# The opening, three seams and the late chunks of a gated two-branch attention kernel dealt anew

## The chip, the cores and the metric

The kernel runs on one core of a Trainium2 chip. Its time is the device time of one execution in microseconds (us), given as the median of several runs. The engines are TensorE (PE, with PEld for its weight loads), VectorE (DVE), ScalarE (ACT), GpSimd (POOL), and SyncE (SP), from whose queue most DMAs are issued.

## The reference

Two attention branches read the same 2048 tokens of width 640 (32 heads of 20) and are mixed by a gate per token.

```python
# first branch: linear attention with softmax features
q, k, v = split_heads(x @ wqkv)
pq, pk = q @ w_phi[h], k @ w_phi[h]                 # 20 x 20 for each head
phi_q = concat(softmax(pq), softmax(-pq))           # phi_k likewise
kv = einsum('sf,sd->fd', phi_k, v); z = phi_k.sum(over s)
a = merge((phi_q @ kv) / (phi_q @ z + 1e-6)) @ A_wo

# second branch: 4 segments of 512 tokens, in order, for each head
p = softmax(q_s @ k_s.T * 20**-0.5 + mask)          # masked where the key comes after the query
phi = lambda t: where(t > 0, t + 1, exp(t))
mem = (phi(q_s) @ M) / (phi(q_s) @ zm + 1e-6)
o_s = sigmoid(beta) * mem + (1 - sigmoid(beta)) * (p @ v_s)
M += phi(k_s).T @ v_s; zm += phi(k_s).sum()
b = merge(o) @ B_wo

g = sigmoid((x * gate_w).sum(-1))
out = g * a + (1 - g) * b                           # 2048 x 640, bf16
```

## The kernel before

A *chunk* is 128 tokens (16 of them), a *half* is 320 of the 640 columns, that is 16 heads: one PSUM bank of float32. The order of instructions on PE, ACT, DVE, POOL and on SP's queue is written out by hand: an engine works through its list in program order, and what stands behind a waiting instruction waits too. Tiles come from pools with a fixed number of slots; a new tile takes the slot that was given back first, and its first writer waits until the readers of the tile before it are done.

*Opening.* The key weights and `w_phi` are folded into one matrix `WkA`: PE transposes the key weights (`emit_foldT`, L173, five groups of five), a block-diagonal `Wphi` is made from `w_phi` and a mask (`emit_Wphi`, L163, five products on DVE), and six products for each of five row blocks (`emit_foldM`, L180) give `WkA`. The tokens must lie transposed: chunks 0 to 3 go through PE (`emit_xT`, L191), the rest through transposing DMAs (`emit_xturn`). The fold's results and the transposed tokens are copied from PSUM by ACT and DVE. POOL meanwhile makes masks and fills `kvn` and `kvd`.

*Key stage* (`emit_a1`, L225, 16 chunks): PE multiplies a chunk by `WkA` (`pk`) and by the value weights (`pv`, with the gate's sum as column 321), ACT takes exp(pk) and exp(-pk) and copies pv, DVE sums and inverts over each head's 20, POOL multiplies (`EkSn`), and a DMA lays the result out in `Z` for the sums z. Then come the fold of the query weights, the sums `kv` over all chunks (L373) and their masked copies `kvn`, while DVE adds the 32 rows of `Z` (`emit_zadd`).

*Query stage* (`emit_pq`, L388): two blocks of 1024 tokens, five product groups of 128 columns each, two slots of PSUM banks wide, exps of both signs by ACT into `Eq`. After the first block PE turns the summed `Z` (`emit_z`, L259) and DVE folds it into `kvd` (`emit_zz`). `kvd` holds for each row block the z values and a column of ones: its product with `Eq` is the numerator's denominator and the softmax's own sum in one. It keeps the 13 heads that a row block touches, and a chunk's denominators take six products of 8 to 24 columns for each sign. Between the fourth and the fifth product group of the second block stand the denominators of chunks 0 to 3 (`den0`), the gate's sigmoid, and two chains of reciprocals and products (`den_chain`), first for chunk 0, then for chunks 1 to 3.

*Numerators* (from L570): for each chunk and sign six products give the numerators (`emit_num`), DVE scales them (`emit_tt`), POOL adds both signs (`oA`, L593), and a transposing DMA puts the result into `oTA` (L606) as weights for the output projection. Denominators of the next four chunks are computed ahead. Between the two signs PE also projects halves of the second branch's keys, queries and values (`emit_next_half`, L566: 32 halves, one at each place until they are used up; ACT copies them to their stages at L552). A key or query chunk of two halves is then turned by a transposing DMA (`emit_turn`). PSUM is dealt as three slots for projections (`pps`), one for denominators (`dps`) and one for each sign's numerators (`nps`).

*Second branch*: 16 double steps, four in each of four segments, each for two groups of four heads. Called d0 to d15 here. A double step has five *bursts*: score products in PSUM (L669), their exponentials on ACT (L673), and the causal zeroing on POOL (`triangles`, L680). Between bursts PE works through a list made from `PLAN`, one letter for one item:

- `h`: a half of the next segment's keys, queries or values, 5 products of 320 columns (L857), copied by DVE (L863)
- `o`: a half of the first branch's output for a chunk from `EARLY` on, 5 products (L803); `f`: a half of the final output. For a chunk below `EARLY` it has 10 products, both branches in one sum; from `EARLY` on it has 5, and DVE adds the kept first-branch half
- `A`, `B`, `C`, `D`: probabilities by values (L725), memory products (L733, L738) and their normalisation
- `x`, `y`: the second part of a feature computation for a key or query chunk (DVE, L832); `z`: turning query features; `t`: turning a chunk of the second branch's output; `u`: the last turns

A piece of `h`, `o` or `f` is one product of 320 columns, and pieces are spread over the bursts by weight. A finished key or query chunk queues its feature exponential (L829, on ACT); the first of the waiting ones is run behind bursts 0 (keys) and 2 (queries). `PLAN` and `FINS` (the order of the final halves) stand in the diff below.

*Tail* (L929 to L988): the last four chunks' outputs, with the first branch's halves added by an identity product.

## Time and profile before

| | |
|---|---|
| runs | 330.01, 330.65, 331.93 us; median 330.65 |
| profiled execution | 330.95 us, of which 329.0 us are the span of the profile |
| granted TensorE clock, mean | 0.997 of full speed |
| instructions in the span | 9567 |
| DMA traffic | 34.21 MB, mean 104 GB/s |
| chain of work that ended last | PE 40%, ACT 18%, issue 2%, DVE 1% of the span |

The span runs from the first instruction to the last on the profiled core; 1.95 us of the execution lie around it. Engines' busy times overlap, and PE's weight loads (PEld) run beside its products. In rows of grouped instructions the part left of the bar is the work (line, engine, operation, result <- operands, shape, count), then busy time and mean length of one (ns), then the engine's idle time just before such instructions and what released most of it. In rows of the timeline the first number is the start in us, the second the length; several instructions alike in a row are one entry, and a bracket tells an idle time ahead of it and its releaser.

### The profile page before, as it was taken

How to read it: one execution, taken by the hardware profiler on the slowest of the kernel's cores; microseconds unless marked ns; L12 is line 12 of the kernel's file. 1: busy time of each engine (PE TensorE's matmuls, PEld its weight loads, DVE VectorE, ACT ScalarE, POOL GpSimd, SP SyncE). 2: the span in 40 equal slices, each digit the busy share in tenths (PEclk: the TensorE clock that was granted, in tenths of full speed). 3: DMA queues.
4: the chain of work that ended last, by engine and by line, in shares of the span. 5: the costliest groups of instructions: out<-in, count | busy, mean ns of one | idle time of the engine just before them, and what ended most of it. 6: DMA issues, size and time to landing. Idle time of an engine off the chain costs nothing.

```text
span 329.0 us, 9567 instructions
## 1 busy us (share of the span) xinstructions
PE 311.3 (95%) x3937; PEld 213.8 (65%) x3940; DVE 224.0 (68%) x449; ACT 252.7 (77%) x320; POOL 210.2 (64%) x306
## 2 busy tenths in 40 slices
PE   7899999999999999799999999999999999999994
PEld 6788877964567787455556566656556666656662
DVE  2477897997788987466768776776666666363552
ACT  3777888229755545799999999999889889889842
POOL 8378689402248889756657667676686768665640
PEclk9999999999999999999999999999999999999998
DMA  7928854692015856558231364843554584612212
GB/s 231 211 67 198 190 129 130 169 369 76 2 18 109 125 110 113 110 97 121 50 59 34 73 102 66 133 73 58 106 87 67 106 107 67 96 47 62 49 63 80
DMA packets 91814, 34.21 MB, mean 104 GB/s; under 512 B 79867, under 2 KB 91771, under 8 KB 91771
## 3 DMA queue, kind: packets, MB, share of 16 engines
q1 hardware_dynamic: 91338, 33.11, 50.1%
q8 instruction: 31, 0.51, 0.7%
q10 hardware_dynamic: 432, 0.49, 0.5%
q14 instruction: 13, 0.10, 0.1%
HBM read 6.42 MB, written 2.62 MB: 27 GB/s over the span
## 4 chain that ended last, share of the span: by engine, by line
PE 40%; ACT 18%; issue 2%; DVE 1%; POOL 0%; ACTq 0%; DVEq 0%
ACT PT L673 16%; PE st_ps L669 10%; PE proj L803 10%; PE nda L725 8%; PE proj L857 6%; PE proj L542 2%; PE nda L733 1%; PE nda L738 1%; PE num L439 1%; PE st_ps L940 1%; ACT ek L829 1%; DVE oTA L951 0%; ACT oTA L948 0%; PE nda L940 0%; DVE rec L752 0%
## 5 line engine op out<-in xcount | busy, mean ns | idle before, releaser
L673 ACT ACTIVATE PT<-st_ps 128x1024 bf16<-128x1024 f32 x160 | 154.3, 1025 | 16.0 <-PE st_ps L669 13.2
L680 POOL TENSOR_SCALAR_AFFINE_SELECT PT<-PT 128x512 bf16<-128x512 bf16 (+1 forms) x130 | 87.0, 687 | 49.3 <-ACT PT L673 49.2
L725 PEld LDWEIGHTS <-PT 128*128 128x128 bf16 x1280 | 39.8, 96 | 11.7 <-issue 8.4
L243 POOL TENSOR_TENSOR EkSn<-Ek,krec 128x1280 bf16<-128x1280 bf16 x16 | 37.7, 2370 | 12.5 <-DVE krec L242 11.9
L725 PE MATMUL nda<-vB,PT 128*128 128x21 bf16 x1280 | 42.8, 173 | 1.2 <-DVE mtmp L768 1.0
L857 PEld LDWEIGHTS <-xTf 128*128 128x128 bf16 x320 | 28.1, 97 | 17.1 <-issue 7.6
L863 DVE CAST Z<-proj 128x320 bf16<-128x320 f32 x48 | 22.8, 487 | 22.1 <-PE proj L857 21.7
L231 PEld LDWEIGHTS <-xTf 128*128 128x128 bf16 x240 | 27.1, 113 | 6.5 <-ACT xTf L196 0.9
L239 DVE TENSOR_REDUCE ksum<-Ek 128x64 f32<-128x1280 bf16 x16 | 23.6, 1475 | 9.2 <-ACT Ek L235 9.2
L669 PE MATMUL st_ps<-Z 32*128 32x512 bf16 (+3 forms) x256 | 24.7, 299 | 4.3 <-ACT PT L673 2.1
L235 ACT ACTIVATE Ek<-pk 128x640 bf16<-128x640 f32 x32 | 20.8, 702 | 10.1 <-PE pk L231 9.3
L803 PE MATMUL proj<-WkA,oTA 128*128 128x320 bf16 x160 | 27.3, 299 | 0.0
L490 DVE TENSOR_TENSOR tt<-num,rr 128x640 f32<-128x640 f32 x32 | 24.7, 801 | 3.3 <-POOL rr L484 2.0
L593 POOL TENSOR_TENSOR oA<-tt 128x640 bf16<-128x640 f32 x16 | 24.6, 1546 | 3.4 <-DVE tt L490 3.0
L669 PE MATMUL st_ps<-Eq 32*128 32x512 bf16 (+3 forms) x256 | 25.1, 299 | 1.4 <-ACT PT L673 0.8
L765 POOL TENSOR_TENSOR oB<-td 128x320 bf16<-128x320 f32 x23 | 19.8, 860 | 6.9 <-DVE td L762 5.6
L398 ACT ACTIVATE Eq<-pq 128x1024 bf16<-128x1024 f32 x20 | 19.4, 1021 | 6.2 <-PE pq L393 4.2
L439 PEld LDWEIGHTS <-Eq 128*128 128x128 bf16 x384 | 19.8, 96 | 4.7 <-issue 1.5
L393 PE MATMUL pq<-xTf,WqA 128*128 128x512 bf16 x97 | 21.9, 379 | 0.7 <-DVE zt L263 0.6
L803 PE MATMUL proj<-WvA,oT 128*128 128x320 bf16 x120 | 22.6, 300 | 0.0
L762 DVE TENSOR_TENSOR td<-nda,rec 128x640 f32<-128x640 f32 x24 | 19.8, 825 | 2.2
L857 PE MATMUL proj<-WqB,xTf 128*128 128x320 bf16 x120 | 20.9, 300 | 0.0
(150 smaller groups left out, 541.6 us busy)
## 6 DMA issues: line engine op xcount, KB each, us to landing
Z<-EkSn SPq DMA_DIRECT2D x32, 160.0 KB, 2.7
out_dram<-orow SPq DMA_DIRECT2D x10, 160.0 KB, 2.0
WvA<-in_A_wqkv_dram SPq DMA_DIRECT2D x2, 400.0 KB, 6.5
WkB<-in_B_wk_dram SPq DMA_DIRECT2D x1, 800.0 KB
WqB<-in_B_wq_dram SPq DMA_DIRECT2D x1, 800.0 KB, 7.0
WvB<-in_B_wv_dram SPq DMA_DIRECT2D x1, 800.0 KB, 10.1
WkA<-in_A_wo_dram SPq DMA_DIRECT2D x1, 800.0 KB, 11.7
WvA<-in_B_wo_dram SPq DMA_DIRECT2D x1, 800.0 KB, 12.8
```

What stands on the lines that cost most here:

```text
L231: nc.tensor.matmul(ps[:, bk, 0:n], lhsT=key_tokens(c, sc), rhs=rhs, start=(c == 0), stop=(c == KC - 1))
L239: nc.vector.tensor_reduce(out=ksum, in_=Ek.rearrange("p s (h f) -> p (s h) f", f=DH), axis=AX.X, op=ALU.add)
L243: nc.gpsimd.tensor_tensor(out=EkSn[:, sc].rearrange("p s (h f) -> p (s h) f", f=DH), in0=Ek.rearrange("p s (h f) -> p (s h) f", f=DH), in1 ...
L439: nc.tensor.matmul(ps(bk, lo, hi), lhsT=Eqs[qb, j][:, sgn, qc * P:(qc + 1) * P], rhs=kvx[:, sgn, j, lo - h0:hi - h0, :].rearrange("p h e - ...
L490: nc.vector.tensor_tensor(out=tt[:, sgn].rearrange("p (b h) d -> p b h d", b=2), in0=ps, in1=csb, op=ALU.mult)
L593: nc.gpsimd.tensor_tensor(out=oA.rearrange("p (h d) -> p h d", d=DH), in0=tt[:, 0], in1=tt[:, 1], op=ALU.add)
L669: nc.tensor.matmul(ps[:, i - i0, o:o + L - c * P], lhsT=kT[32 * i:32 * i + 32, c * P:(c + 1) * P], rhs=qT[32 * i:32 * i + 32, c * P:L], st ...
L673: nc.scalar.activation(out=PT[:, i0:i0 + 2], in_=ps, func=ACT.Exp, scale=SCALE_B)
L680: nc.gpsimd.affine_select(out=v, in_=v, pattern=[[0, n_i], [1, P]], compare_op=ALU.is_ge, fill=0.0, base=0, channel_multiplier=-1)
L725: nc.tensor.matmul(nd[:, j, i], lhsT=block(st, c)[:, i, (j - c) * P:(j - c + 1) * P], rhs=vB[:, c, 4 * st.g + i, :], start=(c == 0), stop= ...
L803: nc.tensor.matmul(ps, lhsT=oT[:, k % KC], rhs=W[:, k % KC, hs], start=(k == 0), stop=(k == n - 1))
L857: nc.tensor.matmul(ps, lhsT=xq[:, sc // 4, k, sc % 4 * P:(sc % 4 + 1) * P], rhs=W[:, k, half * 320:(half + 1) * 320], start=(k == 0), stop ...
```

## The change

- **Opening.** `emit_Wphi` goes from DVE to POOL, ahead of the fills of `kvn` and `kvd`. The transpositions (T), fold products (M) and token transpositions (X) are written out as one sequence in another order. Copies: the fold's results all by ACT (before: even ones by DVE), the token chunks by DVE (before: ACT), the weights' transposed groups by DVE but for the second (before: 0 and 2 by DVE, the others by ACT).
- **Seam of keys and queries.** `kvd` holds all 32 heads for each row block (before: 13), so a sign's denominators of a chunk are five products of 64 columns (before: six of 8 to 24), and `wmask` moves to a pool that lives longer. The turned sums of Z and the first denominators share one tile of two banks, `z_den`. The DVE work on the turned sums (`emit_zz`) is written behind the first product group of the second query block instead of ahead of it.
- **Seam of queries and numerators.** The first denominators' chain is one for four chunks up to the sum, then a reciprocal and two POOL products for chunk 0 and for chunks 1 to 3. It is written behind the last query product group. The PSUM pools are opened in another order, with a pool `last_pps` of one slot taken by every third half, beside `pps` of two.
- **Numerators.** Four more halves, key and query of chunk 4 (the first of segment 1), join the 32; one extra place for a half stands after chunks 4, 9 and 14.
- **Seam of numerators and second branch.** Key and query chunk 4 are turned and their features queued ahead of the loop; in d0 the waiting exponentials run behind bursts 2 (queries) and 3 (keys).
- **Second branch.** `EARLY` goes from 10 to 8: chunks 8 and 9 get their first-branch output halves in segment 0 (places that the four halves leave), and their final halves are of five products. `FINS` and `PLAN` are dealt to fit.

```diff
-    wmask = wq_hold.tile([P, KC, H], F32, name="wmask")
+    wmask = Aw.tile([P, KC, H], F32, name="wmask")
...
-    kvd = Aw.tile([P, 2, KC, HW, 2], BF16, name="kvd")
+    kvd = Aw.tile([P, 2, KC, H, 2], BF16, name="kvd")
...
+    def emit_Wphi(j):
+        h0, h1 = TH[j]
+        nc.gpsimd.tensor_tensor(out=Wphi[:, j, 0:h1 - h0, :],
+                                in0=Wc[:, j:j + 1, :].to_broadcast([P, h1 - h0, DH]),
+                                in1=wmask[:, j, h0:h1, None].to_broadcast([P, h1 - h0, DH]),
+                                op=ALU.mult)
+
+    for j in range(KC):
+        emit_Wphi(j)
...
-        nc.gpsimd.tensor_copy(out=kvd[:, sgn, :, :, 1], in_=wmw)
+        nc.gpsimd.tensor_copy(out=kvd[:, sgn, :, :, 1], in_=wmask)
...
-    def emit_Wphi(j):
-        h0, h1 = TH[j]
-        nc.vector.tensor_tensor(out=Wphi[:, j, 0:h1 - h0, :],
-                                in0=Wc[:, j:j + 1, :].to_broadcast([P, h1 - h0, DH]),
-                                in1=wmask[:, j, h0:h1, None].to_broadcast([P, h1 - h0, DH]),
-                                op=ALU.mult)
-
...
-        eng = nc.vector.tensor_copy if ic % 2 == 0 and dst is WkA else nc.scalar.copy
-        eng(out=dst[:, ic, :].rearrange("p (b n) -> p b n", b=2), in_=ps[:, :, 0:320])
-
-    def emit_xT(sc):
+        nc.scalar.copy(out=dst[:, ic, :].rearrange("p (b n) -> p b n", b=2), in_=ps[:, :, 0:320])
+
+    def emit_xT(sc, eng):
...
-        nc.scalar.copy(out=xq[:, sc // 4, :, sc % 4 * P:(sc % 4 + 1) * P], in_=tp)
+        eng(out=xq[:, sc // 4, :, sc % 4 * P:(sc % 4 + 1) * P], in_=tp)
...
-    def emit_z():
-        zt_ps = aps.tile([P, KC, P], BF16, name="zt_ps", tag="w2")
+    def emit_z(bank):
+        zt_ps = bank.bitcast(BF16)[:, 0:D].rearrange("p (c t) -> p c t", c=KC)
...
+        return zt_ps
+
+    def emit_zz(zt_ps):
...
-
-    def emit_zz():
...
         for sgn in range(2):
-            nc.vector.tensor_tensor(out=kvd[:, sgn, :, :, 0], in0=wmw,
-                                    in1=zcol[:, :, sgn:sgn + 1].to_broadcast([P, KC, HW]), op=ALU.mult)
+            nc.vector.tensor_tensor(out=kvd[:, sgn, :, :, 0], in0=wmask,
+                                    in1=zcol[:, :, sgn:sgn + 1].to_broadcast([P, KC, H]), op=ALU.mult)
...
-    for n in range(KC):
-        emit_foldT(wnat_k, WkT, n, nc.vector.tensor_copy if n in (0, 2) else nc.scalar.copy)
-        if n == 3:
-            for j in range(KC):
-                emit_Wphi(j)
-    for n in range(KC):
-        emit_foldM(WkT, WkA, n)
-        if n in (1, 3):
-            for sc in (n - 1, n):
-                emit_xT(sc)
+    for step in ("T0", "T1", "T2", "M0", "M1", "T3", "T4", "M2", "X0", "M3", "X1", "M4", "X2", "X3"):
+        n = int(step[1])
+        if step[0] == "T":
+            emit_foldT(wnat_k, WkT, n, nc.scalar.copy if n == 1 else nc.vector.tensor_copy)
+        elif step[0] == "M":
+            emit_foldM(WkT, WkA, n)
+        else:
+            emit_xT(n, nc.vector.tensor_copy)
...
-    def emit_pieces(ps, ch, sgn, kvx, e):
+    def emit_num(ch, sgn):
...
+        t = nps.tile([P, 2, 512], F32, name=f"num{sgn}")
...
-            nc.tensor.matmul(ps(bk, lo, hi),
+            nc.tensor.matmul(t[:, bk, (lo - 16 * bk) * DH:(hi - 16 * bk) * DH],
...
-                             rhs=kvx[:, sgn, j, lo - h0:hi - h0, :].rearrange("p h e -> p (h e)"),
-                             start=(n in FIRST) if e > 2 else (n == 0),
-                             stop=(n in LAST) if e > 2 else (n == len(PIECES) - 1))
-
-    def emit_num(ch, sgn):
-        t = nps.tile([P, 2, 512], F32, name=f"num{sgn}")
-        emit_pieces(lambda bk, lo, hi: t[:, bk, (lo - 16 * bk) * DH:(hi - 16 * bk) * DH],
-                    ch, sgn, kvn, DH)
+                             rhs=kvn[:, sgn, j, lo - h0:hi - h0, :].rearrange("p h e -> p (h e)"),
+                             start=(n in FIRST), stop=(n in LAST))
...
     def emit_den(t, ch, k):
+        qb, qc = divmod(ch, HB // P)
         for sgn in range(2):
-            emit_pieces(lambda bk, lo, hi: t[:, k, sgn, lo:hi, :].rearrange("p h e -> p (h e)"),
-                        ch, sgn, kvd, 2)
+            for j in range(KC):
+                nc.tensor.matmul(t[:, k, sgn].rearrange("p h e -> p (h e)"),
+                                 lhsT=Eqs[qb, j][:, sgn, qc * P:(qc + 1) * P],
+                                 rhs=kvd[:, sgn, j].rearrange("p h e -> p (h e)"),
+                                 start=(j == 0), stop=(j == KC - 1))
...
-    def emit_dd(uu, n):
-        dd = emit_dsum(uu, n)
-        nc.vector.reciprocal(out=dd[:, 0:n], in_=dd[:, 0:n])
-        return dd
-
-    def emit_cs(chs, rr, dd):
+    def emit_cs(chs, rr, dd, o=0):
...
-        nc.gpsimd.tensor_tensor(out=dd[:, 0:n], in0=dd[:, 0:n],
+        k = slice(o, o + n)
+        nc.gpsimd.tensor_tensor(out=dd[:, k], in0=dd[:, k],
...
-        nc.gpsimd.tensor_tensor(out=rr[:, 0:n], in0=rr[:, 0:n],
-                                in1=dd[:, 0:n, None, :].to_broadcast([P, n, 2, H]), op=ALU.mult)
-        return rr
+        nc.gpsimd.tensor_tensor(out=rr[:, k], in0=rr[:, k],
+                                in1=dd[:, k, None, :].to_broadcast([P, n, 2, H]), op=ALU.mult)
+        for i, ch in enumerate(chs):
+            cs_of[ch] = rr[:, o + i]
...
-    def den_chain(chs, dt, o):
-        rr, uu = emit_rr(dt, len(chs), o)
-        cs = emit_cs(chs, rr, emit_dd(uu, len(chs)))
-        for k, ch in enumerate(chs):
-            cs_of[ch] = cs[:, k]
+    def first_chain(dt):
+        rr, uu = emit_rr(dt, NB)
+        dd = emit_dsum(uu, NB)
+        for o, chs in ((0, [0]), (1, [1, 2, 3])):
+            nc.vector.reciprocal(out=dd[:, o:o + len(chs)], in_=dd[:, o:o + len(chs)])
+            emit_cs(chs, rr, dd, o)
...
             if (qb, j) == (0, KC - 1):
-                emit_z()
-                emit_zz()
+                z_den = w2tile("z_den")
+                zt_ps = emit_z(z_den[:, 0])
+            if (qb, j) == (1, 0):
+                emit_zz(zt_ps)
...
             if (qb, j) == (1, 3):
-                dt = w2tile("den0").rearrange("p a b -> p (a b)")[:, 0:NB * 4 * H].rearrange(
-                    "p (k s h e) -> p k s h e", k=NB, s=2, e=2)
+                dt = z_den[:, 1].rearrange("p (k s h e) -> p k s h e", k=NB, s=2, e=2)
...
-                emit_gS()
-                den_chain([0], dt, 0)
-                den_chain([1, 2, 3], dt, 1)
+    emit_gS()
+    first_chain(dt)
...
-    pps, dps, nps = [nps_stack.enter_context(tc.tile_pool(name=n, bufs=b, space=bass.MemoryType.PSUM,
-                                                          reuse_waits="tile"))
-                     for n, b in (("pps", 3), ("dps", 1), ("nps", 1))]
+    nps, dps, last_pps, pps = [nps_stack.enter_context(tc.tile_pool(
+        name=n, bufs=b, space=bass.MemoryType.PSUM, reuse_waits="tile"))
+        for n, b in (("nps", 1), ("dps", 1), ("last_pps", 1), ("pps", 2))]
...
-              for half in range(2)]
+              for half in range(2)] + [(part, 4, half) for part in "kq" for half in range(2)]
...
-            emit_half(pps, *halves.pop(0), nc.scalar.copy)
+            emit_half(last_pps if len(halves) % 3 == 1 else pps, *halves.pop(0), nc.scalar.copy)
...
+            if (ch, sgn) in ((4, 1), (9, 1), (14, 1)):
+                emit_next_half()
...
-            cs = emit_cs(ahead, rr_n, dd)
-            for n, c in enumerate(ahead):
-                cs_of[c] = cs[:, n]
+            emit_cs(ahead, rr_n, dd)
...
-        EARLY = 10
+        EARLY = 8
...
-        FIRST_SEG = [(part, c) for c in range(4) for part in "kq"]
-        FINS = [(ch, half) for ch in range(7) for half in range(2)] + [
-            (10, 0), (7, 0), (10, 1), (7, 1), (8, 0), (8, 1), (9, 0), (9, 1), (11, 0), (11, 1)]
+        FIRST_SEG = [(part, c) for c in range(1, 4) for part in "kq"]
+        FINS = [(ch, half) for ch in range(6) for half in range(2)] + [
+            (10, 0), (10, 1), (6, 0), (6, 1), (8, 0), (8, 1), (9, 0),
+            (7, 0), (9, 1), (7, 1), (11, 0), (11, 1)]
...
-        PLAN = {0: ("hhhhhhxAhD", "hhBhyhzChoxAoD", "hoBhyozChoxAoD", "hoBoyozCooxAoD"),
-                1: ("hhBhyhzChhxADtt", "hhBhyhzCfhhxAD", "hhBhyhzCfhhxADt", "hhBhyhzCfhhxAD"),
-                2: ("hhBhyhzCfhhxADt",) * 4,
-                3: ("fByfzCffADtt", "ftBfCftfAD", "fBfCftfAD", "ufBfCfffAD")}
+        PLAN = {0: ("hhhhoyzoAoxD", "hhBhyhzCooxAoD", "hhBhyhzCooxAoD", "ooBoyozCooxAoD"),
+                1: ("hhBhhChxAhDtt", "hhBhyhzCfhhxAD", "hhBhyhzCfhhxADt", "hhBhyhzCfhhxAD"),
+                2: ("hhBhyhzChxAhDt",) + ("hhBhyhzCfhhxADt",) * 3,
+                3: ("fByfzCffADtt", "fBftCfftAD", "fBftCfffAD", "ufBfCfffAD")}
...
+        for part in "kq":
+            emit_turn(part, 4, (kTs if part == "k" else qTs)[1])
+            features(part, 4)
...
-                if n in (0, 2):
-                    run_first(waiting["kq"[n == 0]])
+                if n in ((0, 2) if dstep else (2, 3)):
+                    run_first(waiting["kq"[n == (0 if dstep else 2)]])
...

```

## The prediction

> **What bounds the kernel now.** I read the page first, then busy time in stretches cut at each double step of the second branch (two head groups; d0 to d15), then the order of instructions at the seams.
>
> ```profile
> PE 311.3 (95%) x3937; PEld 213.8 (65%) x3940; DVE 224.0 (68%) x449; ACT 252.7 (77%) x320; POOL 210.2 (64%) x306
> 135.40:145.99 10.59, 9.66 (x111) 5.37 (x111) 4.85 (x11) 9.99 (x11) 5.36 (x8) 1.00 0.59 107
> 168.32:179.48 11.16, 10.62 (x158) 6.62 (x157) 8.31 (x20) 10.72 (x12) 7.23 (x13) 1.00 0.26 48
> 179.48:190.44 10.96, 10.18 (x157) 6.32 (x156) 8.14 (x18) 10.51 (x12) 7.33 (x15) 1.00 0.49 69
> 225.07:236.80 11.73, 11.48 (x172) 7.21 (x171) 7.56 (x18) 10.24 (x12) 9.03 (x17) 1.00 0.41 76
> 271.63:283.00 11.37, 11.30 (x167) 7.17 (x166) 6.30 (x14) 10.21 (x12) 9.03 (x17) 1.00 0.49 80
> 283.00:293.77 10.77, 10.64 (x157) 6.55 (x155) 4.80 (x10) 9.69 (x11) 6.45 (x11) 1.00 0.51 73
> ```
>
> The stretches read: limits, length, then PE, PEld, DVE, ACT, POOL busy, clock, DMA share, GB/s. They are d0, d3, d4, d8, d12, d13. TensorE is busy 95% overall, but the owner changes: in d3 and d4 ACT is busier than PE (10.72 against 10.62, 10.51 against 10.18), while in d8, d12 and d13 PE leads ACT by 0.95 to 1.24 us. So a product taken from d8 or d13 shortens them; in segment 0 it does not, and there an exponential counts. The clock is 1.00 throughout.
>
> **The opening.** Columns: start, length, instruction.
>
> ```profile
> 0.81 0.46 SPq L97 DMA_DIRECT2D Wc<-in_A_w_phi_dram  x1
> 2.58 0.71 POOL L141 COPY wmw<-wmask 128x12 f32<-128x12 f32 x5
> 6.67 0.73 PE L176 MATMUL wtp<-ident_b,wnat_k 128*128 128x128 bf16 x10 [0.79 <-DMA wnat_k<-in_A_wqkv_dram]
> 7.25 1.27 PE L184 MATMUL fold_ps<-Wphi,WkT 128*128 128x240 bf16 x12
> 10.89 1.33 ACT L196 COPY xTf<-xtp 128x640 bf16<-128x640 bf16 x2
> 12.28 1.55 PE L231 MATMUL pk<-WkA,xTf 128*128 128x320 bf16 x10 [0.85 <-ACT xTf L196]
> Wc<-in_A_w_phi_dram SPq DMA_DIRECT2D x1, 25.0 KB, 2.8
> L484 POOL TENSOR_TENSOR rr<-rr,dd 128x64 f32<-128x64 f32 x1 | 0.3, 317 | 0.1
> L484 POOL TENSOR_TENSOR rr<-rr,dd 128x256 f32<-128x256 f32 x3 | 2.2, 727 | 0.2
> L178 DVE COPY WkT<-wtp 128x640 bf16<-128x640 bf16 x2 | 1.0, 490 | 5.4 <-PE wtp L176 5.4
> ```
>
> The five products that make Wphi go from DVE to POOL, ahead of the kvn fills. POOL is free at 3.29 and Wc lands at 0.81 + 2.8 = 3.6. POOL has no such product in the trace; the nearest are its broadcast products, 317 ns at 64 and 727 at 256 columns, so 2.1 ns a column over 0.18 us. Wphi has 240 + 140 + 260 + 140 + 140 = 920 columns: 1.9 + 0.9 = 2.8 us, ready at 6.4 to 6.5. The fold's first product then ends near 6.7 instead of about 7.75 (half of the twelve from 7.25). From there to the first key product the kernel before takes 4.5 us; the new order adds the last two transposition groups (about 0.56 of the 0.73 shown), which had stood idle for 0.79 waiting for their weights and now come after two fold products, and takes away most of the closing wait: the last token copy is one on DVE, 0.49, where ACT did two in series in 1.33. So 4.5 + 0.56 - 0.5, the key stage starts at 11.3: **-0.9**. Ends: -1.2 (both idle stretches gone), and +0.3 if POOL takes 4 us for Wphi. POOL's later fills and the two wider kvd copies are hidden: its first key product came at 17.4. The key stage that follows is PE without a gap, so the shift is kept.
>
> **The query seam.**
>
> ```profile
> 58.15 8.02 PE L373 MATMUL kv_ps<-vA,EkSn 128*128 128x140 bf16 x128
> 81.05 8.79 PE L393 MATMUL pq<-xTf,WqA 128*128 128x512 bf16 x39 [0.58 <-DVE zt L263]
> 88.19 0.37 DVE L272 TENSOR_TENSOR kvd<-wmw,zcol 128x65 bf16<-128x65 f32 x2
> 89.68 1.35 PE L439 MATMUL den<-kvd,Eq 128*128 128x24 bf16 x48
> 93.04 0.56 PE L439 MATMUL num<-kvn,Eq 128*128 128x240 bf16 x6
> 95.23 0.84 PE L542 MATMUL proj<-WkB,xTf 128*128 128x320 bf16 x5 [0.43 <-ACT Eq L398]
> 95.23 1.49 DVE L490 TENSOR_TENSOR tt<-num,rr 128x640 f32<-128x640 f32 x2
> 96.51 0.56 PE L439 MATMUL num<-kvn,Eq 128*128 128x240 bf16 x6
> L461 DVE RECIPROCAL rr<-den 128x64 f32<-128x64 f32 x1 | 0.6, 558 | 2.0 <-PE den L439 2.0
> L461 DVE RECIPROCAL rr<-den 128x192 f32<-128x192 f32 x1 | 1.3, 1295 | 0.0
> ```
>
> First, the transposed sums now lie in half of a tile that the denominators fill later, so the next query product takes another slot and waits for no DVE copy: **-0.6** (0.58 shown). What is late next is the kvd product: it ended at 88.56 while PE reached the denominators at 89.68; with PE 0.6 earlier and the products 160 columns wide (two at perhaps 0.1 us more), 88.8 still precedes 89.1. If that margin is gone it costs up to 0.3.
>
> Second, the denominators are 160 products of 64 columns where there were 192 of 8 to 24. No row has 64. The 48 take about 25 ns each (1.20 us to the next query product), the 128 of 140 columns 63. So 160 x 25 to 160 x 63 against 192 x 25 = 4.8: -0.8 to +5.3 us over the stage; 64 lies nearer to 24 than to 140, and in line between them 38 ns; products that stream their columns fall below that line near the floor, and I take 30: **0**. The Trainium skill (TensorE: Matmul & The Clock Gate, "Wait — 56ns, not 53.3ns?") gives a floor of about 25 ns and columns divided by 2.4 GHz plus 2.5 ns; by that estimate 64 columns take 29 ns and the term is -0.1.
>
> Third, the banks of the numerators. The second projection waited until 95.23 for the last query exponential, 2.19 after the first numerator at 93.04. Now the slot of that exponential belongs to the denominators' bank, and the first projection's to the first chain. That chain is one reciprocal of 256 (from 558 and 1295: 1.67 us), a product and a sum, and the first tt needs only a short second reciprocal: DVE reaches it near 94.7 instead of 95.23. PE runs numerator, projection, numerator, projection (0.4, 0.68, 0.4, 0.68) to 95.2 where the last exponential is just done, denominators of 0.6 follow, and the second chunk's numerator comes 2.8 after the first instead of 3.47: **-0.65**. At worst the first projection waits for the chain's uu and 0.3 of it stays.
>
> **The numerators and the seam to the second branch.**
>
> ```profile
> 114.42 0.56 PE L439 MATMUL num<-kvn,Eq 128*128 128x240 bf16 x6 [0.30 <-DVE tt L490]
> 125.29 0.68 PE proj L542 x5
> 131.55 1.26 SPq L556 DMA_TRANSPOSE Z<-Z  x1
> 132.68 0.84 PE L542 MATMUL proj<-WvB,xTf 128*128 128x320 bf16 x5
> 132.91 3.90 SPq L606 DMA_TRANSPOSE oTA<-oA  x3
> 134.97 0.40 PE L669 MATMUL st_ps<-Z 32*128 32x512 bf16 x4 [1.45 <-ACT vB L552]
> 138.97 0.64 PE L669 MATMUL st_ps<-Z 32*128 32x256 bf16 x8
> Z<-Z SPq DMA_TRANSPOSE x16, 3.3
> ```
>
> Four half projections come in, 5 products and 0.68 us each: 2.7 us of PE. ACT copies them with half its time free. One after chunk 4: +0.68. One after chunk 9: it fills a stall of 0.30 like that at 114.42 (DVE ends late in each batch), +0.38. Two stand at the end. There PE finished at 133.4 and began the second branch only at 134.97. The row puts that on an ACT copy that was long done; what lands then is the transposition of the last query chunk, issued at 131.55, 3.3 later: 134.85. That transposition hangs on the POOL sum of chunk 12, not on PE, so the two halves fill the hole. From chunk 9 on PE now needs 0.38 + 1.36 more against 1.57 of room: +0.2. Together **+0.9**; +2.7 if nothing hides.
>
> On SP the transposition of key chunk 4 now stands ahead of that of the last first-branch chunk, and query chunk 4 behind it; two of its kind leave the queue of d0 in exchange. The first output piece of d0 waits for the former: POOL sum near 136.3, issue 1.3, landing 2.7 after the issue began, so about 139.1 to 139.5, while PE comes to it near 139.7 (after 138.97 and the rest of the half). I add **+0.2**, ends 0 and 0.7.
>
> **The second branch.**
>
> ```profile
> 181.31 0.74 ACT L829 ACTIVATE ek<-Z 128x640 bf16<-128x640 bf16 x1
> 181.93 3.77 ACT L673 ACTIVATE PT<-st_ps 128x1024 bf16<-128x1024 f32 x4
> ```
>
> In segment 0 four halves leave and four output halves of chunks 9 and 8 come: 35 pieces in each of d0 to d3, as before. d0 gets a second feature exponential, 0.62 on ACT (181.31 to 181.93), and becomes like d3: 10.59 to 11.16, **+0.6**. d4 loses one: 10.96 - 0.62 = 10.34, PE's 10.18 below it: **-0.5**. d8 loses an output half of ten pieces, worth 1.2 (d12 with 40 against d13 with 35: 0.60 for five) to 1.37 by 0.137 each; ACT's 10.24 is just below 11.73 - 1.37: **-1.2**. The output halves of chunks 8 and 9 are now five pieces instead of ten: d12 and d14 keep 40 and 35; d13 goes 35 to 30 and d15 40 to 35: **-0.65** each. Their adds on DVE cost what the copies did, with DVE half idle (4.80 in d13).
>
> Sum: -0.9 - 0.6 + 0 - 0.65 + 0.9 + 0.2 + 0.6 - 0.5 - 1.2 - 1.3 = **-3.45 us**. The profiled execution is 330.95 us, 0.30 above the median 330.65: 327.5 against its own time, **327.2** against the median.
>
> **The rivals.**
> - The opening gains nothing: Wphi on POOL is late, or the value weights hold the first pv. Without the 0.9 it is 328.1. Against it: POOL would need 1 us more than its nearest rows say.
> - ACT holds the steps that lose pieces, and the halves cost PE as they come in: without d8, d13 and d15 (2.5) the time is 329.7, with half the seam's cover gone too 330.6: no change. For it: ACT is over 85% busy there. Against: d13 was shorter than d12 by its five pieces with ACT at 9.69 and 10.21.
> - Slower: d0's first output piece waits. PE is in order, so every score product behind it waits too and ACT runs dry. If the transpositions run one after another, each for its full 2.7 to 3.3 us, then from 131.55: 134.9, 137.6, 140.3, 143.6 and the wanted one at 146.3, 6.6 after PE gets there: 333.8. It ends in a loss above 330.65 + 1.65 once the wait passes 5.1 us. Against: three were issued in 3.90 us, and those before were used by PE without a wait.
>
> **How the numbers follow.** My forecast has 0.66, the opening rival 0.12, no gain in the second branch 0.14, the wait in d0 0.08. About 0.5%, 1.65 us, is what can be told from no change. Faster: nearly all of the first and most of the second, 0.75; same 0.17; slower 0.08. The range takes the terms' better ends (opening -1.2, halves +0.6, d8 -1.37, the rest as they are, and 0.7 spread) at 325.8, and reaches up to 330.2, into the no-gain rival; the forecast's own range is 325.8 to 328.9.
>
> **What would show it.** Right: the first key product near 11.3; no wait of pq for zt; second chunk's numerator 2.8 after the first; under 0.5 us of idle PE before the first score product; d4 near 10.4, d8 near 10.5, d13 near 10.1. Wrong: POOL's Wphi past 7.5; a denominator product above 40 ns; PE waiting for oTA in d0; d8 above 11.2.

## The result and the profile after

The changed kernel takes 329.16 us (median of 9 runs, 329.01 to 330.23) against 330.65; the ratio of the two is 0.9959, 95% interval 0.9944 to 0.9974. The forecast was 327.2: the sign was right, the gain was 1.5 us instead of 3.45. The profiled execution takes 329.01 us with a span of 327.3, 1.94 us less than the one before. Of the runs behind the times of this document one, of the kernel late_only below, ran at a mean granted clock of 0.682; it took 407.57 us and is left out of that kernel's ratio.

First the page's busy line and busy time in stretches of the changed kernel (limits, length, then PE, PEld, DVE, ACT, POOL, clock, DMA share, GB/s); the stretches are d0, d4, d8, d12, d13 and d14, each from a step's first exponential to the next step's.

```profile
PE 309.1 (94%) x3905; PEld 213.3 (65%) x3908; DVE 222.5 (68%) x444; ACT 252.2 (77%) x321; POOL 212.3 (65%) x311
133.89:144.58 10.69, 9.57 (x109) 5.29 (x109) 5.50 (x11) 10.46 (x12) 5.07 (x8) 1.00 0.81 153
178.17:188.92 10.75, 10.23 (x156) 6.31 (x154) 6.31 (x16) 10.17 (x11) 6.94 (x15) 1.00 0.66 80
223.55:235.74 12.19, 10.11 (x162) 6.36 (x161) 7.28 (x17) 10.10 (x11) 9.43 (x18) 1.00 0.39 68
270.32:281.68 11.36, 11.29 (x167) 7.16 (x165) 6.30 (x14) 10.20 (x11) 9.03 (x17) 1.00 0.20 47
281.68:291.97 10.29, 9.75 (x150) 6.07 (x149) 4.84 (x10) 9.58 (x11) 6.28 (x10) 1.00 0.34 81
291.97:303.12 11.15, 10.30 (x155) 6.45 (x155) 5.35 (x11) 9.52 (x10) 6.58 (x10) 1.00 0.27 69
```

For d14 the kernel before has this row:

```profile
293.77:304.67 10.90, 10.80 (x158) 6.74 (x157) 5.00 (x10) 9.69 (x11) 6.65 (x11) 1.00 0.17 48
```

d8 is the odd one. It has ten products of 320 columns less, PE's busy time fell by 1.37 as forecast, and the step became 0.46 longer: neither PE nor ACT fills it. d14, whose products did not change in number, grew by 0.25 with PE's busy time half a microsecond smaller.

Start times of the same event in the two profiles show where the shift was won and lost (the shifts are differences of unrounded times):

| event | before | after | shift |
|---|---|---|---|
| first fold product | 7.25 | 5.45 | -1.79 |
| first key product | 12.28 | 10.57 | -1.71 |
| first query product | 69.23 | 67.81 | -1.42 |
| first denominator | 89.68 | 87.51 | -2.17 |
| first numerator | 93.04 | 90.83 | -2.20 |
| second chunk's numerator | 96.51 | 93.60 | -2.90 |
| last chunk's last numerator product | 132.62 | 131.18 | -1.44 |
| first score product | 134.97 | 133.46 | -1.51 |
| d4, d5 | 179.48, 190.44 | 178.17, 188.92 | -1.31, -1.52 |
| d8, d9, d10 | 225.07, 236.80, 248.61 | 223.55, 235.74, 247.29 | -1.52, -1.06, -1.32 |
| d14, d15 | 293.77, 304.67 | 291.97, 303.12 | -1.80, -1.54 |
| end of the span | 328.99 | 327.30 | -1.69 |

At the second chunk's numerator 2.9 us are won. The halves and the seam behind them take 1.4 of it, and the whole second branch, from which the forecast took 2.2, brings 0.18. d9 is shorter by 0.26, so d8 and d9 together lost 0.20.

The timeline of the changed kernel at the opening, at the query seam, and at the start of the second branch (start, length, instruction):

```profile
3.60 2.32 POOL L144 TENSOR_TENSOR Wphi<-Wc,wmask 128x240 bf16<-128x240 bf16 x5 [0.30 <-DMA Wc<-in_A_w_phi_dram]
5.45 1.26 PE L186 MATMUL fold_ps<-Wphi,WkT 128*128 128x240 bf16 x12
10.57 1.55 PE L232 MATMUL pk<-WkA,xTf 128*128 128x320 bf16 x10 [0.60 <-DVE xTf L197]
87.51 1.33 PE L450 MATMUL z_den<-kvd,Eq 128*128 128x64 bf16 x40
90.83 0.56 PE L440 MATMUL num<-kvn,Eq 128*128 128x240 bf16 x6
93.60 0.56 PE L440 MATMUL num<-kvn,Eq 128*128 128x240 bf16 x6
103.32 0.75 PE L450 MATMUL den<-kvd,Eq 128*128 128x64 bf16 x20
103.90 0.56 PE L440 MATMUL num<-kvn,Eq 128*128 128x240 bf16 x6
130.15 1.26 SPq L553 DMA_TRANSPOSE Z<-Z  x1
133.46 0.40 PE L666 MATMUL st_ps<-Z 32*128 32x512 bf16 x4 [0.70 <-issue]
```

Twenty denominator products take 0.58 us (103.32 to 103.90), 29 ns each. The first score product still finds PE idle for 0.70 us; the turn of the last query chunk was issued at 130.15 and lands some 3.3 later.

Then d8 and d14 of the changed kernel, the waits that their rows above hide:

```profile
231.04 3.26 SPq L839 DMA_TRANSPOSE xTf<-Eq  x2
231.74 0.76 PE L722 MATMUL nda<-vB,PT 128*128 128x21 bf16 x24 [0.74 <-DVE mtmp L765]
234.96 0.21 PE L730 MATMUL nda<-Mbd,xTf 128*128 128x84 bf16 x1 [0.82 <-DMA xTf<-Eq]
300.25 0.57 PE L800 MATMUL proj<-WvA,oT 128*128 128x320 bf16 x3 [0.54 <-DVE oTA L809]
```

In d8 the last of the memory products for the first group waits 0.82 us for the turned query features of chunk 11, and the products by values wait 0.74 for the normalisation of the group before. In d14 an output product waits 0.54 for one of the two PSUM slots, which DVE has not yet emptied.

### The profile page after: what moved, and what is told of

It is laid out like the page before. It is cut to its first block, busy times and chain, and to the rows that moved or that the text cites. A ratio compares the mean times of both kernels' runs of the same rounds, so it can differ in the third digit from the quotient of the medians.

```text
span 327.3 us, 9498 instructions
## 1 busy us (share of the span) xinstructions
PE 309.1 (94%) x3905; PEld 213.3 (65%) x3908; DVE 222.5 (68%) x444; ACT 252.2 (77%) x321; POOL 212.3 (65%) x311
## 4 chain that ended last, share of the span: by engine, by line
PE 39%; ACT 21%; DVE 2%; issue 2%; DMA 1%; SPq 0%; ACTq 0%; DVEq 0%
ACT PT L670 19%; PE st_ps L666 9%; PE proj L800 8%; PE proj L854 6%; PE nda L722 6%; PE proj L539 4%; PE num L440 2%; DMA xTf<-Eq 1%; PE nda L730 1%; PE nda L735 1%; PE st_ps L941 1%; ACT ek L826 1%; DVE oTA L952 0%; ACT oTA L949 0%; PE den L450 0%
## 5 line engine op out<-in xcount | busy, mean ns | idle before, releaser
L854 PEld LDWEIGHTS <-xTf 128*128 128x128 bf16 x300 | 26.3, 97 | 16.0 <-issue 7.2
L860 DVE CAST Z<-proj 128x320 bf16<-128x320 f32 x44 | 20.8, 486 | 20.1 <-PE proj L854 19.8
L232 PEld LDWEIGHTS <-xTf 128*128 128x128 bf16 x240 | 27.1, 113 | 6.2 <-DVE xTf L197 0.7
L236 ACT ACTIVATE Ek<-pk 128x640 bf16<-128x640 f32 x32 | 20.8, 702 | 10.6 <-PE pk L232 9.8
L539 PEld LDWEIGHTS <-xTf 128*128 128x128 bf16 x180 | 16.3, 97 | 4.4
L747 DVE RECIPROCAL rec<-nda 128x32 f32<-128x32 f32 (+1 forms) x32 | 10.6, 330 | 12.4 <-PE nda L730 6.5
```

The source lines that it names most:

```text
L232: nc.tensor.matmul(ps[:, bk, 0:n], lhsT=key_tokens(c, sc), rhs=rhs, start=(c == 0), stop=(c == KC - 1))
L539: nc.tensor.matmul(ps, lhsT=xq[:, sc // 4, cc, sc % 4 * P:(sc % 4 + 1) * P], rhs=W[:, cc, half * 320:(half + 1) * 320], start=(cc == 0), s ...
L854: nc.tensor.matmul(ps, lhsT=xq[:, sc // 4, k, sc % 4 * P:(sc % 4 + 1) * P], rhs=W[:, k, half * 320:(half + 1) * 320], start=(k == 0), stop ...
```

## The experiments

The theory after the result: the opening and the query seams gained more than forecast; the rest was lost at two kinds of place, transpositions whose landing PE now reaches too early (ahead of d0 and in d8), and two-slot output halves. The main rival: the gains in the first branch cannot pass the seam at d0, whatever is done there, and the second branch is bound by ACT.

Medians, with the ratio to the kernel before on the same chip (330.59 us for the first four, 330.47 for the next four, 330.80 for the last two):

| kernel | us | ratio, 95% interval |
|---|---|---|
| seams_only | 329.03 | 0.9946 (0.9929 to 0.9964) |
| opening_only | 328.94 | 0.9944 (0.9925 to 0.9963) |
| late_only | 331.38 | 1.0021 (1.0009 to 1.0034) |
| turn_early | 328.54 | 0.9936 (0.9915 to 0.9957) |
| d8_replan | 328.08 | 0.9923 (0.9901 to 0.9946) |
| fins_spread | 328.91 | 0.9946 (0.9925 to 0.9966) |
| q3_first | 328.76 | 0.9940 (0.9919 to 0.9961) |
| wphi_dve | 331.26 | 1.0015 (0.9996 to 1.0035) |
| seams_q3 | 326.82 | 0.9877 (0.9859 to 0.9896) |
| best1 | 326.91 | 0.9876 (0.9859 to 0.9893) |

### The opening alone

opening_only is the kernel before with the first item of the change, all else as it was.

```diff
+    for j in range(KC):
+        emit_Wphi(j)
     for sgn in range(2):
         nc.gpsimd.memset(kvn[:, sgn], 0.0)
...
+    for step in ("T0", "T1", "T2", "M0", "M1", "T3", "T4", "M2", "X0", "M3", "X1", "M4", "X2", "X3"):
...
```

> The kernel before with the new opening alone (Wphi on POOL, the new order of transpositions, fold products and token turns, and their copies). First theory: the first key product comes at 10.6 instead of 12.3 and the shift of 1.7 us is kept to the end, 328.95. Rival, the size in the prediction: 0.9 kept, 329.75, because the key stage or the sums behind it give the rest back (the changed kernel lost 0.33 of it at the masked copies of kv).

328.94 us: 1.65 us, the first theory's number, and within the intervals as much as the whole change brings. In its own profile the first key product comes at 11.25, since the weights landed late there:

```profile
7.50 0.73 PE L178 MATMUL wtp<-ident_b,wnat_k 128*128 128x128 bf16 x10 [0.57 <-DMA wnat_k<-in_A_wqkv_dram]
11.25 1.55 PE L232 MATMUL pk<-WkA,xTf 128*128 128x320 bf16 x10 [0.59 <-DVE xTf L197]
```

Over the profiles with the new opening that start lies between 10.50 and 11.25 us. So the opening's worth is read from medians, and starts further on are compared counted from the first query product. This profile does not show one shift kept from end to end: of the 1.03 us at the first key product 0.73 are left at the first query product (68.50 against 69.23), and 0.30 come back in d9, which takes 11.51 instead of 11.81.

### Where Wphi is made

```diff
-        nc.gpsimd.tensor_tensor(out=Wphi[:, j, 0:h1 - h0, :], ...
-    for j in range(KC):
-        emit_Wphi(j)
+        nc.vector.tensor_tensor(out=Wphi[:, j, 0:h1 - h0, :], ...
...
+        if step == "M0":
+            for j in range(KC):
+                emit_Wphi(j)
```

> The changed kernel with the five products that make Wphi on DVE again, issued ahead of the first fold product, all else of the new opening kept. First theory: the opening gained 1.7 us instead of the forecast 0.9 because Wphi's first parts were ready on POOL at 4.1 to 5.4, and the order and the copies bring little; with Wphi behind two copies on DVE the fold starts near 7.3, the first key product comes near 12.0 and the time is 330.5. Rival: order and copies bring the gain, wherever Wphi is made; first key product near 11.0 and 329.5.

```profile
7.37 0.28 PE L183 MATMUL fold_ps<-Wphi,WkT 128*128 128x240 bf16 x1 [0.90 <-DVE Wphi L144]
12.91 0.33 PE L229 MATMUL pk<-WkA,xTf 128*128 128x320 bf16 x1 [0.60 <-DVE xTf L194]
```

Nearer the first theory: fold at 7.37, first key product at 12.91, 331.26 us, with the kernel before inside the interval. The new order with a late Wphi is worse than expected, since PE then waits in order for three of the parts (0.90, 0.28 and 0.21 us). So without Wphi's early place nothing of the gain is left. An early Wphi in the old order was not run, so what the order itself adds to it is not shown.

### The parts apart

seams_only has the opening and the two query seams, and everything from the halves on as before. late_only is the reverse: the kernel before with the halves, the early turns, `EARLY`, `FINS` and `PLAN` of the change. From the changed kernel to seams_only:

```diff
-              for half in range(2)] + [(part, 4, half) for part in "kq" for half in range(2)]
+              for half in range(2)]
-            if (ch, sgn) in ((4, 1), (9, 1), (14, 1)):
-                emit_next_half()
-            emit_half(last_pps if len(halves) % 3 == 1 else pps, *halves.pop(0), nc.scalar.copy)
+            emit_half(last_pps if len(halves) % 3 == 0 else pps, *halves.pop(0), nc.scalar.copy)
-        EARLY = 8
+        EARLY = 10
...
-            emit_turn(part, 4, (kTs if part == "k" else qTs)[1])
-            features(part, 4)
...
-                if n in ((0, 2) if dstep else (2, 3)):
+                if n in (0, 2):
```

> The opening and the two query seams of the change, with the 32 halves, the output halves and the step lists of the kernel before. First theory: the shifts add up. The second chunk's numerator came 2.9 us earlier in the changed kernel (93.60 against 96.51), and what stood at 1.5 at the first score exponential was lost to the extra halves alone; so without them d0 starts near 132.5 and the time is 330.65 - 2.9 = 327.7. Rival: the transpositions and the POOL sums ahead of d0 set its start, whatever PE gains before; then d0 starts near 133.9 again and the time is 329.1 to 329.3.

> The kernel before with the late part of the change alone: four more halves among the numerators, chunk 4 turned ahead of the loop, the output halves of chunks 8 and 9 early, the new step lists. First theory: the extra halves cost 1.4 us up to d0's start and the second branch gives back 0.2, so this kernel is slower than before, 331.85. Rival: the halves are cheap and it is the earlier seams that collide with them; then it is no slower than before, 330.0 to 330.7.

seams_only comes out at 329.03, near the rival's number, though d0's first exponential at 133.35 lies between the two theories. It is no faster than the opening alone: 2.54 us ahead of the kernel before at the second chunk's numerator, 2.05 at the first score product, 1.20 at d1. Its timeline, and its busy time in a stretch behind the wait:

```profile
129.66 1.26 SPq L553 DMA_TRANSPOSE Z<-Z  x1
132.92 0.40 PE L664 MATMUL st_ps<-Z 32*128 32x512 bf16 x4 [2.02 <-issue]
133.25 2.53 PE L852 MATMUL proj<-WkB,xTf 128*128 128x320 bf16 x9
133.00:136.70 3.70, 3.70 (x23) 1.62 (x23) 0.49 (x1) 2.28 (x3) 1.70 (x2) 0.55 0.46 92
```

PE is idle for 2.02 us ahead of d0, and then nine products take 2.53 us, for which the kernel before needs 1.40: the granted clock is 0.55 in that stretch. From the first query product to the second chunk's numerator the query seams win 1.48 us (25.80 against 27.28). Of that, 0.5 are lost by the first score product, where PE stands idle for 2.02 instead of 1.45, and the slow clock behind it takes 0.84 more from d0 (11.44 against 10.60). Of the runs of this kernel the two with a mean clock of 0.999 took 328.61 and 328.65, the others, at 0.993 to 0.995, 328.98 to 329.46.

late_only is 0.8 us slower than the kernel before, between the two theories and nearer the first. Its first score product comes 1.3 us later counted from the first query product, and the second branch gives 0.7 back. Its d8:

```profile
226.06:237.28 11.22, 9.83 (x158) 6.19 (x157) 7.28 (x17) 9.98 (x12) 8.64 (x16) 1.00 0.36 68
```

d8 takes 11.22 there, though the feature turn is issued later in the step than in the changed kernel (7.93 us after its start against 7.49): it landed sooner. d8 took 12.1 to 12.2 in the changed kernel and in the three variants below that keep its list (fins_spread, q3_first, wphi_dve).

The DMA packets of the traces show what differs. A transfer of 16384 bytes, on the queue that the page of the profile lists as `q8 instruction`, starts while this turn is under way in six of the twelve profiles: the kernel before, opening_only, the changed kernel and the three variants. There the turn takes 3.75 to 3.94 us from issue to landing. In the other six the transfer falls outside the turn, which then takes 2.26 to 2.39. No run moves this transfer alone, so that it delays the turn is likely but not shown.

### The turn ahead of d0

```diff
-        nc.sync.dma_start_transpose(out=oTA[:, ch], in_=oA)
+        held = [] if ch != 13 else held
+        held.append((ch, oA))
+        for c_, o_ in held if ch != 12 else ():
+            nc.sync.dma_start_transpose(out=oTA[:, c_], in_=o_)
```

This puts the turn of query chunk 3 ahead of the transposition of first-branch chunk 12 on SP's queue, which waits for a POOL sum. q3_first has it on the changed kernel, seams_q3 on seams_only.

> The changed kernel with one transposition moved on SP's queue: that of first-branch chunk 12 stands behind the turn of the last query chunk of segment 0 instead of ahead of it. First theory: d0's first score product waits for this turn (0.70 us of idle PE at 133.46, the turn issued at 130.15 and landing 3.3 later), and the turn is issued 1.3 us sooner; PE starts d0 at 132.8 and the time falls by 0.7 to 328.45. Rival: the transpositions run one after another in the DMA engines, so the turn lands no sooner, or d0 gives the 0.7 back; 329.15.

> The kernel of the opening and the two query seams alone (329.03, without the late part) with the last query chunk's turn ahead of the transposition of first-branch chunk 12 on SP's queue. First theory: what the query seams gained, 1.4 us at the second chunk's numerator, was lost only because PE stood idle for 2.02 us ahead of d0 for this turn and then ran at half the granted clock for 3.4 us (1.1 us lost in d0). The turn's data were ready at 127.0 and it was issued at 129.7; issued at 127.4 it lands at 130.7, where PE ends its last half at 130.9. Then hole and half clock both go: d0 of 10.6 again instead of 11.4, and a time of 326.4 to 327.2. Rival: the turn is only the last of several things that d0 waits for (the DMA engines, POOL's sums), and another one holds it within half a microsecond of the old place; the half clock stays, 328.7 to 329.0.

q3_first: 328.76; PE has no idle time ahead of d0 any more, and the first score product comes 0.77 earlier counted from the first query product:

```profile
133.28 0.39 PE L669 MATMUL st_ps<-Z 32*128 32x512 bf16 x4
```

The time fell by 0.4, within the noise of the two intervals. The profile carries that verdict: from the first query product to the end of the span it takes 258.71 us against 259.49, so the 0.77 is kept.

seams_q3: 326.82, 2.2 us less than without the edit. Its timeline:

```profile
125.78 3.46 SPq L553 DMA_TRANSPOSE Z<-Z  x2
131.28 0.40 PE L667 MATMUL st_ps<-Z 32*128 32x512 bf16 x4 [0.72 <-DVE tt L486]
131.60 1.40 PE L855 MATMUL proj<-WkB,xTf 128*128 128x320 bf16 x9
```

The two turns go out together from 125.78, the hole is 0.72 instead of 2.02, the nine products take 1.40 again and d0 10.60. So the loss at this seam was one transposition's place in a queue, and the slow clock was its consequence.

### d8

The list of d8 in turn_early, and then in d8_replan:

```diff
-                2: ("hhBhyhzChxAhDt",) + ("hhBhyhzCfhhxADt",) * 3,
+                2: ("hhByzhhChxAhDt",) + ("hhBhyhzCfhhxADt",) * 3,
```
```diff
-                2: ("hhBhyhzChxAhDt",) + ("hhBhyhzCfhhxADt",) * 3,
+                2: ("hhByzhhChhxADt",) + ("hhBhyhzCfhhxADt",) * 3,
```

> The changed kernel with one edit in d8: the query features of chunk 11 are finished and their turn is issued ahead of the query halves of chunk 12, not between and behind them. PE's order is the same. First theory: d8 is held by PE's wait for this turn (0.82 us at the fourth memory product), since taking ten pieces out moved the second query half, and with it the turn, one burst later; the wait goes, d8 falls from 12.2 to about 11.4 and the time to 328.4. Rival: ACT's exponentials and POOL's zeroing set d8, and the wait is only where PE idles anyway; d8 stays above 12.0 and the time at 329.2.

> The changed kernel with d8's list changed in two ways: the query features of chunk 11 and their turn ahead of the query halves, and two halves instead of one between the end of the step before (C) and the first products by values (A). First theory: besides the turn, PE in d8 waits 0.74 us for the normalisation on DVE behind C, because only five pieces stand in between where twenty did; with both waits gone d8 falls from 12.2 to 10.5, and the time to 327.7 (without the second edit d8 was 11.22 and the time 328.5). Rival: ten exponentials and one feature exponential, 11.0 us of ACT with the gaps between them, set d8; then it stays at 11.2 and the time at 328.5.

Busy time in d8, first of turn_early, then of d8_replan:

```profile
223.46:234.68 11.22, 9.83 (x158) 6.19 (x157) 7.09 (x17) 9.99 (x12) 8.77 (x16) 1.00 0.46 86
```
```profile
223.28:234.25 10.97, 10.17 (x161) 6.39 (x160) 6.99 (x17) 9.99 (x11) 8.88 (x17) 1.00 0.47 90
```

With PE's order untouched and only the turn issued earlier, d8 falls from 12.19 to 11.22: the wait was real, not a place where PE would have idled. d9 takes 0.21 of it back (11.76 against 11.55). The time is 328.54, as the first theory had it, though its interval overlaps with the changed kernel's. The second edit takes the 0.74 away too but gains 0.25 in d8, not 0.7, and 0.19 in d9; that is between the theories. PE's idle times in d8 are then 0.17, 0.34 and 0.28 us, and each ends with an exponential of ACT. d8_replan's 328.08 is 1.1 us below the changed kernel, with intervals that still touch.

The turn was issued late because of the pieces that were taken out. Items are dealt to the five bursts by weight, so with ten pieces less each burst takes fewer. The second query half, of which the kernel before had all but one product done in the second burst, slid into the third. Its own turn stands ahead of the feature turn on SP's queue, and was issued 6.20 us after the step's start where the kernel before has 5.67. In the kernel before, then in the changed one:

```profile
230.74 1.23 SPq L556 DMA_TRANSPOSE Eq<-Z  x1
```
```profile
229.75 1.24 SPq L553 DMA_TRANSPOSE Eq<-Z  x1
```

The late issue alone is not enough: late_only issues the turn later still, and where it lands in 2.4 us PE does not wait.

### The final halves of d14

```diff
-            (10, 0), (10, 1), (6, 0), (6, 1), (8, 0), (8, 1), (9, 0),
+            (10, 0), (10, 1), (6, 0), (8, 0), (6, 1), (8, 1), (9, 0),
```

> The changed kernel with the final halves of d14 in another order: five, ten, five pieces by turns, where three halves of five pieces followed one another. First theory: DVE adds such a half only when the normalisation ahead of it is done, PE runs out of its two slots and waits 0.54 us in d14; spread out, the wait goes, d14 falls from 11.15 to 10.7 and the time by 0.4 to 328.75. Rival: ACT's exponentials set d14 in any case; d14 stays at 11.1 and the time at 329.15.

The first identity product of the tail, in the changed kernel and in this one:

```profile
313.70 0.30 PE L936 MATMUL st_ps<-oTA,ident_b 128*128 128x320 bf16 x1
```
```profile
312.96 0.30 PE L936 MATMUL st_ps<-oTA,ident_b 128*128 128x320 bf16 x1
```

PE's wait for DVE in d14 is gone, and its 0.54 us comes out, but only by the end of d15: 0.74 at the tail's first product, of which 0.21 stood at d14's start already. Read between first exponentials d14 went only from 11.15 to 11.07; most of the gain appears behind the last exponential of d15. In the time, 328.91, such a size cannot be told from nothing.

### All three repairs

> The changed kernel with the three repairs together: d8's new list (-1.1 measured alone), the final halves of d14 spread out (-0.25), the last query chunk's turn ahead of one transposition (-0.4). First theory: they lie in three separate places, so they add up, 327.4. Rival: the wait that one repair takes away comes back in the next (d15 and the tail wait for DVE or the DMA turns anyway); 327.9 to 328.1.

326.91 us: 2.25 below the changed kernel, 0.5 better than the sum of the three. One wait is new, in d0:

```profile
138.78 0.99 PE L803 MATMUL proj<-WkA,oTA 128*128 128x320 bf16 x6 [0.70 <-DMA oTA<-oA]
```

This is the wait of the forecast's slower rival: the first output piece reaches the transposition of the last first-branch chunk too early. It did not occur in the changed kernel, where PE came to this piece 0.4 us later (138.45 against 138.08), nor in q3_first, which has the same order on SP's queue. There the two turns ahead of d0 were issued in 3.31 us, in best1 in 3.98, and all that stands behind them came later. In q3_first, then in best1:

```profile
127.03 3.31 SPq L553 DMA_TRANSPOSE Z<-Z  x2
```
```profile
126.66 3.98 SPq L553 DMA_TRANSPOSE Z<-Z  x2
```

With this wait d0 takes 11.03 instead of 10.69. Whether every run of best1 has it is not known. best1 is no faster than seams_q3, which has none of the late part: once the seam ahead of d0 is mended, the halves, `EARLY` and the new plans bring nothing that these runs can tell (each interval reaches about half a microsecond to either side), even with d8 and d14 mended as well.

## Why the prediction was right and wrong

The forecast was 2.0 us too low. The start of d0 came out a little better than forecast (-1.51 against -1.25 at the first score product), so the miss lies in the second branch, which was to bring 2.2 and brought 0.18. The step that failed is the one on d8: it took the ten products off the step's length and did not ask when the turned query features land, for which PE then waited 0.82 us, besides 0.74 for DVE. It alone is off by 1.7 us; the other terms miss by less and partly cancel.

- **Opening, -0.9: mis-sized, with more gain than forecast.** (The forecast's own 11.3 against 12.28 makes it -1.0.) Wphi's price on POOL was too high: five products took 2.32 us instead of 2.8. And the fold needs them part by part, so it began at 5.45 while the last part was still to come, where I had waited for all. The first key product came 1.71 earlier. 0.3 of that went at the masked copies of kv, for which PE waits 0.80 us instead of 0.47; I had taken the way to the query stage for one without a gap. Alone the part is worth 1.65.
- **The zt wait, -0.6, and the second chunk's numerator 2.8 behind the first: right.** The first denominator moved by 0.75 against the first query product, and the second chunk came 2.77 behind the first.
- **Denominators, 0: right.** 29 ns each. The Trainium skill's figure (TensorE: Matmul & The Clock Gate, "Wait — 56ns, not 53.3ns?"), 64 columns over 2.4 GHz plus 2.5 ns, gives the same.
- **Halves, +0.9 up to d0: right only beside the hole.** Counted from the first query product they cost 0.90 against seams_only (65.65 against 64.75), which stands idle for 2.02 us there. On the old seams they cost 1.3 (late_only), and with the hole mended in both kernels 1.4 (q3_first against seams_q3). The hole ahead of d0 was rightly put down to the turn issued at 131.55 behind the POOL sum of chunk 12, but used only to hide two halves in. It also meant that what the query seams gain can end at this turn, for which the forecast has no term: seams_only loses 0.5 of their 1.48 us there, and 0.84 more to the slow clock behind it.
- **d0, +0.6 and +0.2: wrong in size.** It grew by 0.1, though ACT's busy time grew by 0.47 (9.99 to 10.46): the second feature exponential fits where ACT had waited for PE, 0.4 us ahead of d1's first exponential. No wait for the transposition came.
- **d4, -0.5: less than half.** -0.21. Why not more was not looked into.
- **d8, -1.2: wrong, the largest miss.** It grew by 0.46, past the forecast's own sign of being wrong. The price of ten products was applied to a step where a turn lands about 11 us after the step's start (10.90 in the kernel before, 11.36 in the changed one, with the transfer of 16384 bytes inside the turn in both). In the kernel before the four memory products take 0.48 us there, where they take 0.31 in the step before it, so the landing was already about to be met; and fewer pieces moved the turn later. With the turn issued early the step takes 11.22 (turn_early), with the wait for DVE gone too 10.97 (d8_replan); the forecast 10.5 was not reached.

```profile
224.19 0.31 PE L733 MATMUL nda<-Mbd,xTf 128*128 128x84 bf16 x4
235.74 0.48 PE L733 MATMUL nda<-Mbd,xTf 128*128 128x84 bf16 x4
```

- **d13 and d15, -1.3: a third of it.** -0.48 in d13, +0.25 in d14, -0.14 in d15 and the tail. "Their adds cost what the copies did" leaves out the two slots: halves of five pieces ask for a slot twice as often, and in d14 a normalisation of about 1.8 us on DVE stands in front of the add. fins_spread shows 0.5 of the missing 0.9 to be this wait. In d13 and d15 PE waits for ACT's exponentials, 0.44 and 0.70 us in all, where the kernel before has no such wait above 0.15; no run takes these waits away alone.

The rival "no gain in the second branch" named the place where the forecast failed. Its cause, ACT, is not what held d8, but PE's waits in d13 and d15 fit it. The changed kernel's 329.16 lies below its 329.7 mostly because d0 grew by 0.1 and not by 0.8.

## What to carry to other kernels

Before a product is taken out of a step, look for what in that step comes by DMA at a fixed time after its start, and whether the dealing of items moves that DMA's issue. Time won upstream can end at the next wait on a queue: read which instruction stands ahead of the late transfer, and move that first. One transposition's place on SP's queue was worth 2.2 us on seams_only, more than the whole change, and 0.4 on the changed kernel.

## What the runs showed of the hardware

In seams_only an idle TensorE of 2.02 us ahead of d0 was followed by 3.4 us at half the granted clock (0.55 over the stretch above), while 1.45 us in the kernel before and 0.70 in the changed one were not. The Trainium skill (TensorE: Matmul & The Clock Gate, "What's actually happening") has the clock fall after an idle window of about 3.4 us and return after a busy one of that length, with windows that run freely. The length of the slow stretch agrees with the trace; the fall came after less idle time, and by the mean clocks not in two of that kernel's six runs.

The same DMA turn of d8 took 2.26 to 2.39 us from issue to landing in six profiles and 3.75 to 3.94 in the six where a transfer of 16384 bytes on the queue `q8 instruction` started while it was under way. The place of that transfer differs between kernels: 8.3 us after d8's start in the kernel before, 9.3 in the changed one, 6.4 in late_only, 10.6 in seams_only.
